# RWKV-7 recurrence and exact-GELU MLP on one core: one hand-written table of single-engine steps in place of loops and calls

## The chip, the cores and the metric

The kernel runs on one core of a Trainium2 chip. The metric is the device time of one execution, in microseconds (us), the median over runs. The engines of the core are named as in the profile: PE (TensorE matmul) with PEld (its weight loads), DVE (VectorE), ACT (ScalarE), POOL (GpSimd), and the queue SP (SyncE), which in this kernel issues nearly all DMAs.

## The reference

A recurrence over 768 time steps, for 4 batches and 8 heads with a state of 40 by 40, and then an MLP on its output. Cut to what matters:

```python
for t in range(S):                                   # S = 768; B, H, D = 4, 8, 40
    y[:, :, t] = einsum('bhd,bhde->bhe', rt, state)
    Sa = einsum('bhde,bhe->bhd', state, at)
    state = state * wt[:, :, None, :] - einsum('bhd,bhe->bhde', Sa, bt) \
            + einsum('bhd,bhe->bhde', vt, kt)
x = y.transpose(0, 2, 1, 3).reshape(B * S, H * D)    # 3072 x 320
h = x @ w_in                                         # w_in 320 x 2048, w_out 2048 x 320, both float64
out = (0.5 * h * (1 + erf(h / sqrt(2)))) @ w_out
```

## The kernel before, in words

Time is cut into 12 chunks of 64 steps. All arithmetic is float32. A chunk c has these parts.

- **Inputs.** SP loads w, a, b, k, v and r of the chunk. Chunks 0 to 2 (for b and k 0 to 3) come as rows of 160 bytes and are turned by PE against an identity; later chunks come in pairs and are turned by DVE.
- **Decays** (`logs`, `sums`). ACT takes the logarithm of w, PE sums it along time (`wT_ps` and `cum`), ACT takes exponentials. DVE and POOL scale a, b and k by them (`scale_a`, `scale_b`, `scale_k`).
- **Masked products** (`make_N`, `make_A`, `make_RV`). 32 small matmuls each on PE, a mask on DVE.
- **The inverse of a triangular matrix.** For chunk 0 by squarings on PE (`squares`). For the others N goes to DRAM (`make_N`, L617), comes back as blocks (L672), POOL inverts the blocks of 32 column by column (`start_inverse`, L680 and L682), the result goes to DRAM (`store_inverse`, L694) and back (`fetch_inverse`, L704 and L708). DVE turns a block of it (`turn_corner`, L780), and PE makes the off-diagonal block in two products, J and its second half (`corner`, `joined`).
- **The state.** `make_av` and `make_X` (PE, tile XA), copies, `make_sa` (PE, tile S), a mask on DVE, `make_QY` (PE, the state products), `outputs` (DVE additions into the state and into xt, the MLP's input, with some rows of xt moved by eleven small DMAs on SP), `turn_state` and `make_y2`.
- **The MLP.** `mlp` makes, for each quarter of the hidden width, two groups of ten matmuls and one exact GELU on ACT into the tile gt (L986, L988). The second product is plain in chunks 0 to 2 (L1003) and from chunk 3 on takes seven half-size products for eight (`seven`, L939), with additions on DVE. The result is stored from the tile os.

The weights are float64, and the chip has no such arithmetic: `to_float` builds a float32 from the two 32-bit words. There are 26 pieces, ten of `w_in` (128 x 512) and sixteen of `w_out` (128 x 320). Each takes bit operations on DVE and one ACT operation (L321 to L326) and is ended either by DVE (L329, L330) or by ACT and POOL together (L332 to L335). The words of `w_in` are landed in the tiles of `w_out`, of gt and in a spare tile (`first_load`, L379 to L388), those of `w_out` in several places (`second_load`, L403), some of them issued by ACT's queue.

The order of the instructions of each engine is the order of the program's calls, and each engine takes its own in that order: an instruction that waits holds everything behind it on its engine or queue. For chunks 0 and 1 the calls are written out one by one; for chunks 2 to 11 a loop (L1229) makes them. MLP pieces of the chunk before are put between by `fill()`, each a quarter of the hidden width (20 matmuls of 256 columns each for x), or one product. Five matmul groups on constants (`keep`) and three before the first input (`warm`) compute nothing that is used. All PE results go through a ring of four PSUM tiles (`duo`), used strictly in turn. Most small matmuls have line L110, that of the helper `mm`; flips have L461, masks L577.

```python
    def fill(n=1):                                   # L1017
        while n and pieces:
            if next(pieces[0], "end") == "end":
                pieces.pop(0)
            else:
                n -= 1
...
    for c in range(2, NCH):                          # L1229, cut
        n, n2 = c + 1, c + 2
        corner(c); make_av(c); make_y2(c); fill(); make_X(c); fill()
        load_next(n2); joined(c); scale_b(n); fill(); make_sa(c)
        ...
        make_QY(c); outputs(c); pieces.append(mlp(c)); fill()
        make_A(n); sums(n2); turn_state(); fetch_inverse(n)
        ...
        make_N(n2); start_inverse(n2, nc.gpsimd); load_kb(n2); load_VR(n2)
```

Of the kernel before, what the change touches and what calls it, by code (L numbers as in the profile page):

```python
# [15 lines left out]

@with_exitstack
def kernel(  # L20
# [12 lines left out]

    nc = tc.nc
# [15 lines left out]
    REST = HP - D  # L83

    const = ctx.enter_context(tc.tile_pool(name="const", bufs=1))
    work = ctx.enter_context(tc.tile_pool(name="work", bufs=1))
    dram = ctx.enter_context(tc.tile_pool(name="scr", bufs=2, space=bass.MemoryType.DRAM))
    psum = ctx.enter_context(tc.tile_pool(name="psum", bufs=4, space=PSUM))

    asked = []  # L90

    def keep(columns):

        asked[:] = [columns]

    def duo(name):
        pt = psum.tile([P, 2, 512], FP32, tag="duo", name=name)
        while asked:
            n = asked.pop()
            mm(pt[:, 0, :n * P], ident, cum_m.unsqueeze(1).to_broadcast([P, n, P]))  # L100
        return pt
# [3 lines left out]

    def head_of(i, x):
        return 2 * i + x
# [5 lines left out]
    def ring(name, n, shape, zero, eng):  # L113
        tiles = []
        for i in range(n):
            t = const.tile(shape, FP32, name=f"{name}{i}")
            if zero is not None:
                eng.memset(zero(t), 0.0)
            tiles.append(t)
        turn = [0]  # L120

        def take():
            turn[0] += 1
            return tiles[(turn[0] - 1) % n]
        return take
# [4 lines left out]
    def whole(t):  # L130
        return t


    def unused(t, eng):
        for x in range(2):
            eng.memset(t[x * HP + BL:(x + 1) * HP, :, BW - BL:D + BL], 0.0)


    NT = 3

    NB = 4
    NS = 3
    paired = {n: const.tile([P, G * H, BW], FP32, name=n + "_pairs") for n in ("a", "v", "r")}
    w_tile = const.tile([P, G * DM + REST], FP32, name="w_tile")


    extra = const.tile([P, 4 * G * H * HP], FP32, name="extra")
    b_rows, k_rows = ([const.tile([P, G * DM + REST], FP32, name=f"{n}_rows{i}") for i in range(2)] for n in "bk")

    def rows(t):  # L150
        return t[:, :G * DM].rearrange("p (g h d) -> p g h d", g=G, h=H)

    raws = {}

    def rows_of(src, c, e):

        return src[G * e:G * (e + 1), :, c * C:(c + 1) * C, :].rearrange("g h t d -> t (g h) d")
# [1196 lines left out]
```

## Time and profile before

| what | value |
|---|---|
| time, three runs | 714.62, 717.1, 721.06 us; median 717.1 |
| span of the profiled execution, first to last instruction | 712.0 us (the page gives no other time for it; the median is 5.1 us above) |
| PE busy | 659.8 us, 93% |
| PEld busy | 574.9 us, 81% |
| DVE busy | 373.2 us, 52% |
| POOL busy | 353.3 us, 50% |
| ACT busy | 229.9 us, 32% |
| mean granted PE clock | 0.965 |
| DMA | 74.25 MB in 287910 packets, 104 GB/s |

How to read it: the page shows one profiled execution. "Busy" is the time in which at least one instruction of the engine was running. The slices row cuts the span into 40 equal parts, each digit the busy share in tenths. In a timeline a row has start and length in us, engine, line, operation, and in brackets how long the engine stood idle before it and what ended that. A PE row of "x40" counts each float32 matmul twice, since it is done in two passes.

### The profile page before, as it was taken

The numbers are of one execution on the slowest core, as the hardware profiler recorded it, in microseconds if no ns is written. First come the engines' busy times: TensorE is split into PE (matmuls) and PEld (weight loads), VectorE is DVE, ScalarE is ACT, GpSimd is POOL, SyncE is SP. The second block draws the span as 40 slices with busy tenths as digits, with TensorE's granted clock in tenths as the row PEclk, the third lists the DMA queues.
The fourth block names the chain that finished last, engine by engine and source line by source line (L and its number), as shares of the span: only waits on it lengthen the run. The fifth ranks groups of instructions, "written<-read, shape, count | busy, mean of one in ns | idle before, by whom it ended". The sixth has DMA issues, their size and how long they took to land.

```text
span 712.0 us, 29566 instructions
## 1 busy us (share of the span) xinstructions
PE 659.8 (93%) x13240; PEld 574.9 (81%) x13240; DVE 373.2 (52%) x484; ACT 229.9 (32%) x306; POOL 353.3 (50%) x796
## 2 busy tenths in 40 slices
PE   7577896789999999999998999999999999999997
PEld 4476685667777877899897798998898898998887
DVE  2325768994262482683582573672771862712303
ACT  5123873453141242242332332333323323111020
POOL 4384458800862862863844823855837818800000
PEclk9777899789999999999999999999999999999999
DMA  9699539764667557557657446647748553120100
GB/s 130 118 168 154 100 99 199 121 129 85 124 121 117 118 102 127 116 100 133 126 94 135 94 94 126 131 90 133 138 83 153 109 102 66 23 51 3 29 9 19
DMA packets 287910, 74.25 MB, mean 104 GB/s; under 512 B 265736, under 2 KB 284456, under 8 KB 287784
## 3 DMA queue, kind: packets, MB, share of 16 engines
q1 hardware_dynamic: 283360, 68.20, 52.5%
q0 software_dynamic: 864, 2.36, 2.0%
q10 hardware_dynamic: 3560, 1.80, 1.3%
q8 instruction: 104, 1.70, 1.1%
q14 instruction: 22, 0.18, 0.1%
HBM read 58.69 MB, written 9.70 MB: 96 GB/s over the span
## 4 chain that ended last, share of the span: by engine, by line
PE 79%; DVE 6%; ACT 3%; DMA 3%; issue 3%; SPq 3%; POOL 2%; ACTq 1%; DVEq 0%; POOLq 0%
PE ph L986 28%; PE po L939 18%; PE po L1003 6%; PE XA L110 5%; PE QY L110 4%; PE J L110 2%; PE S L110 2%; PE sq L110 2%; PE RV_ps L110 2%; PE N_ps L110 2%; SPq L163 2%; PE Y L110 1%; PE tn_ps L461 1%; PE A_ps L110 1%; DMA VR<-in_v_dram 1%
## 5 line engine op out<-in xcount | busy, mean ns | idle before, releaser
L986 PE MATMUL ph<-xt,w_in_sb 64*128 64x256 f32 x1920 | 223.6, 386 | 4.8 <-ACT kT L544 4.8
L986 PEld LDWEIGHTS ph<-xt,w_in_sb 64*128 64x128 f32 x1920 | 185.3, 190 | 30.0 <-ACT kT L544 5.2
L680 POOL TENSOR_TENSOR tmp<-W,Nb 128x126 f32<-128x126 f32 (+22 forms) x310 | 128.3, 414 | 157.8 <-DMA Nb<-N 134.9
L682 POOL TENSOR_TENSOR W<-W,tmp 128x126 f32<-128x126 f32 (+22 forms) x310 | 131.4, 424 | 24.3
L988 ACT ACTIVATE gt<-ph 128x1024 f32<-128x1024 f32 x48 | 49.2, 1024 | 180.7 <-PE ph L986 180.7
L939 PE MATMUL po<-w_out_sb,gt 128*128 128x160 f32 x576 | 82.8, 302 | 1.3 <-DVE gt L959 1.3
L939 PEld LDWEIGHTS po<-w_out_sb,gt 128*128 128x128 f32 x576 | 78.8, 190 | 3.3 <-DVE gt L959 1.5
L1003 PE MATMUL po<-w_out_sb,gt 128*128 128x320 f32 x192 | 53.9, 436 | 0.0
L827 DVE COPY SM<-XA 128x832 f32<-128x832 f32 x10 | 10.3, 1025 | 78.9 <-PE XA L110 78.9
L1003 PEld LDWEIGHTS po<-w_out_sb,gt 128*128 128x128 f32 x192 | 35.7, 190 | 14.7 <-issue 0.3
L836 DVE TENSOR_TENSOR SM<-S,upper 128x832 f32<-128x832 f32 x24 | 23.5, 1019 | 33.9 <-PE S L110 33.9
L794 ACT COPY Js<-J 128x256 f32<-128x256 f32 x11 | 4.1, 373 | 85.4 <-PE J L110 85.4
L810 DVE COPY Tt<-J 32x512 f32<-32x512 f32 x9 | 6.2, 689 | 42.6 <-ACT Tt L810 42.6
L901 ACT COPY st<-apart 128x640 f32<-128x640 f32 x11 | 8.0, 726 | 55.1 <-DVE apart L900 55.0
L939 PE MATMUL po<-extra,half 128*128 128x160 f32 x176 | 25.4, 299 | 0.0
L879 DVE TENSOR_TENSOR st<-QY,st 128x832 f32<-128x832 f32 (+1 forms) x22 | 20.8, 986 | 8.4 <-PE QY L110 8.4
L322 ACT ACTIVATE conv<-conv,rebias 128x320 uint32<-128x320 uint32 (+1 forms) x26 | 15.9, 623 | 28.0 <-DVE conv L321 23.8
L991 DVE TENSOR_TENSOR half<-gt 128x1024 f32<-128x1024 f32 x9 | 11.3, 1260 | 25.8 <-ACT gt L988 25.8
L939 PEld LDWEIGHTS po<-extra,half 128*128 128x128 f32 x176 | 24.2, 190 | 0.0
L110 PE MATMUL XA<-VR,A 64*64 64x104 f32 x768 | 22.5, 270 | 0.0
L577 DVE TENSOR_TENSOR N<-N_ps,upper 128x1024 f32<-128x1024 f32 x12 | 14.7, 1221 | 13.4 <-PE N_ps L110 13.4
L670 POOL MEMSET W<- 128x512 f32 x10 | 5.3, 530 | 32.6 <-DMA inv<-W 32.6
(208 smaller groups left out, 1107.5 us busy)
## 6 DMA issues: line engine op xcount, KB each, us to landing
Nb<-N SPq DMA_DIRECT2D x20, 256.0 KB
VR<-in_v_dram SPq DMA_DIRECT2D x24, 160.0 KB
out_dram<-os SPq DMA_DIRECT2D x48, 80.0 KB
b_rows<-in_b_dram SPq DMA_DIRECT2D x22, 160.0 KB
k_rows<-in_k_dram SPq DMA_DIRECT2D x22, 160.0 KB
N<-N SPq DMA_DIRECT2D x44, 64.0 KB
Tt<-inv SPq DMA_DIRECT2D x44, 64.0 KB
a_pairs<-in_a_dram SPq DMA_DIRECT2D x18, 144.0 KB
```

The source lines that it names most:

```text
L110: nc.tensor.matmul(o, lhsT, rhs, start=first, stop=True, skip_group_check=True)
L163: eng.dma_start(out=t[half(e)].rearrange("p g h d -> p (g h) d")[:, :, :D], in_=rows_of(src, c, e))
L322: nc.scalar.activation(power, power, ACT.Relu, bias=rebias, scale=8.0)
L577: nc.vector.tensor_tensor(to, pt, upper.unsqueeze(1).to_broadcast([P, 2 * G * NP, C]), ALU.mult)
L680: eng.tensor_tensor(t, W[:, :rows, j:j + 1].to_broadcast([P, rows, rest]), Nb[:, j:j + 1, j + 1:].to_broadcast([P, rows, rest]), ALU.mult)
L682: eng.tensor_tensor(W[:, :rows, j + 1:], W[:, :rows, j + 1:], t, ALU.add)
L836: nc.vector.tensor_tensor(SM[:, g], S[g].rearrange("p x i c -> p i x c"), pass_upper.unsqueeze(1).unsqueeze(1).to_broadcast([P, NP, 2, VC] ...
L879: nc.vector.tensor_tensor(given[g][:, :, :, cols], t["QY"][g][:, :, :, cols], given[g][:, :, :, cols], ALU.add)
L939: nc.tensor.matmul(po[:, n, :DM // 2], l_[:, f], r_[:, f], start=f == 0, stop=f == NF // 2 - 1)
L986: nc.tensor.matmul(ph[:, x, s], w_in_sb[half(x), kt, p * P:(p + 1) * P], xt[half(x), kt], start=kt == 0, stop=kt == NK - 1)
L988: nc.scalar.activation(gt[:, 4 * q:4 * q + 4].rearrange("p (x s) t -> p x s t", x=2), ph, ACT.Gelu)
L1003: nc.tensor.matmul(po[:, g], gt[:, f, g * P:(g + 1) * P], w_out_sb[:, f], start=f == 0, stop=f == NF - 1)
```

## The change

Nearly the whole text of the kernel is rewritten. The arithmetic is the same. Each part above is cut into **steps** that run on one engine (or are one DMA group on one queue), a table lists all steps of all chunks in one order, and a loop performs them. A name has the step, the chunk and at times a part: `mh.3.6` is piece 6 of 8 of chunk 3's first MLP product.

- PE: `wT`, `cu` (the two sums), `ta tb tk tv tr` (flips of a, b, k, v, r), `nm am vm` (the products N, A, RV), `qm` (squarings), `jm km` (J and its second half), `av xm` (XA), `sm` (S), `pk pb` (state products), `tm ym`, `mh` (first MLP product, now 10 matmuls to a step where `fill` gave 20), `pm` (a quarter of the second product), `m1` to `m7`.
- DVE: `sb sa` (scaled b, a), `nk ak vk` (masks), `qz qa` (squarings), `tc_` (the turned block), `sc` (mask of S), `oa om od` (state, xt, decayed state), `s1` to `s4`, `e2 e4 e5 e6`, and of the conversions `cp cm cs cv`. The number of a conversion step is its unit: 0 to 9 are `w_in`, 10 to 25 `w_out`.
- ACT: `lg ew en ec`, copies, `ge` (GELU), `ce cl cn` of the conversions.
- POOL: `ic` (columns of the inverse, in groups), `iz`, `sk` (scaled k), `cg` (end of a conversion).
- DMA, a last letter giving the queue (s for SP if none): `L` steps (`Lw La Lb Lk LV Lv Lr` inputs, `Lf Lfe Lf5` words of `w_in`, `Ls` units of `w_out`), `Ns Nl` (N out and back), `Is If Ij` (inverse out and back), `ox` (rows of xt), `so` (store).

The core of the diff: the loop, the `keep` calls, the pools with rotating tiles and the generators go; in come fixed tiles, four PSUM tiles handed out in the order in which they come free, and the table.

```diff
-    psum = ctx.enter_context(tc.tile_pool(name="psum", bufs=4, space=PSUM))
-    def keep(columns):
-        asked[:] = [columns]
-    def duo(name):
-        pt = psum.tile([P, 2, 512], FP32, tag="duo", name=name)
-        while asked:
-            n = asked.pop()
-            mm(pt[:, 0, :n * P], ident, cum_m.unsqueeze(1).to_broadcast([P, n, P]))
-        return pt
-    for c in range(2, NCH):
-        ...
-    fill(1000)
+    banks = [psum.tile([P, 2, 512], FP32, name=f"bank{i}") for i in range(4)]
+    idle, held, left = list(range(4)), {}, {}
+    def take(name, readers=1):
+        held[name] = idle.pop(0)
+        left[name] = readers
+        return bank(name)
+    def drop(name):
+        left[name] -= 1
+        if not left[name]:
+            idle.append(held.pop(name))
+    @step
+    def mh(c, p):
+        q, s = p // 2, p % 2
+        ph = (bank if s else take)(f"ph{c}_{q}").rearrange("p x (s t) -> p x s t", s=2)
+        for kt in range(NK):
+            for x in range(2):
+                nc.tensor.matmul(ph[:, x, s], w_in_sb[half(x), kt, p * P:(p + 1) * P], xt[half(x), kt],
+                                 start=kt == 0, stop=kt == NK - 1)
+    for token in order(NCH, NS):
+        perform(steps, token)
```

The landing places of the words: `w_in`'s first half in the tiles of `w_out` and its second half in gt, as before, but its last unit now in xt; `w_out`'s units in the tiles of `w_out`, gt and the second row tiles of b and k:

```diff
+    def first_home(kt, part):
+        if part == 0:
+            return flat_out[:, kt * LW:(kt + 1) * LW]
+        return flat_xt[:, :LW] if kt == NK - 1 else flat_gt[:, kt * LW:(kt + 1) * LW]
+    def second_home(f):
+        n = 2 * DM
+        if f < 8:
+            return flat_out[:, f * n:(f + 1) * n]
+        if f in (8, 14):
+            return b_rows[1][:, :n].bitcast(UINT32)
+        if f in (9, 15):
+            return k_rows[1][:, :n].bitcast(UINT32)
+        if f == 13:
+            return flat_out[:, 7 * n:8 * n]
+        at = NF // 2 * TB + (f - 10) * n
+        return flat_gt[:, at:at + n]
```

The table begins so, and a later stretch (chunks 5 and 6) reads:

```
Lw.0 lg.0 La.0 Lf.0.1.1 Lb.0 pads_a.0 identity pads_rows.0 first_ones.0 pads_w.0 pads_extra.0
pads_extra.1 sums_mask cu.0 ec.0 sb.0 Tt_zero pads_a.1 upper_mask wT.0 tb.0 sn.0 ew.0 ta.0 sa.0 nm.0 nk.0
Lw.1 first_ones.1 iz.1 qt lg.1 cu.1 pads_VR.0 pads_w.1 pads_VR.1 pads_rows.1 bias_set Lf.1.1.0 Lf.0.0.0
Lf.0.1.0 Lf.1.1.1 Lf.0.0.1 Lf.1.0.0 Lf.1.0.1 Lk.0 Lfe.0 pads_extra.2 qi qm.0 cl.2 warm_set cp.0
warm_first cp.1 cm.0 ce.0 ce.1 qc.0 ec.1 cs.0 qz.0 qm.1 qc.1 cv.0 cm.1 cl.1 cn.1 qa.1 qz.1 cm.2 La.1
Lfe.1 Lr.0 Lb.1 Lf.2.1.1 Lf5.0.1 Lf.3.1.1 Lf5.0.0 Lf.2.1.0 Lf.3.0.1 Lf.3.0.0 LV.0 Lf.2.0.1 Lf.3.1.0
Lf.2.0.0 pads_r.0 sk.0.p wT.1 qm.2 cs.1 cp.2 sb.1 ew.1 cn.2 ce.2 cl.3 cs.2 cg.1 cm.3 cg.2 qc.2 tk.0 tb.1
...
Ls.14 Nl.2.1 La.3 Nl.2.0 Lw.3 ge.0.2 cn.22 cl.22 cp.22 ce.22 cs.22 cg.22 ge.0.3
...
e2.4 e4.4 e5.4 e6.4 LV.7 LV.6
ox.5.0 nm.7 av.6 ym.6 If.6.1 Ij.6.0 nk.7 Ij.6.1 La.8 If.6.0 tc_.6 yc.6 mh.5.2 jm.6 xm.6 jc.6 km.6 kt0.6
mh.5.3 xc0.6 kt1.6 xc1.6 sm.6 sc.6.1 mh.5.6 sc.6.0 mh.5.7 mh.5.0 mh.5.1 mh.5.4 mh.5.5 so.4.1 Ns.7.0
```

Counted over the program: matmuls 6715 (before 6720), SP's DMAs 756 (746), ACT's DMAs 6 (16), ACT table loads 41 (34), POOL's two-tensor operations 719 (711), DVE's scalar-operand operations 128 (136). The three warm matmuls stand behind the first squaring.

## The prediction

> **What bounds the kernel now.** I read the page's busy shares first, then the table of stretches, the timelines of TensorE (PE) and of the SP queue, and last the round trip of one chunk's inverse.
>
> ```profile
> span 712.0 us, 29566 instructions
> PE 659.8 (93%) x13240; PEld 574.9 (81%) x13240; DVE 373.2 (52%) x484; ACT 229.9 (32%) x306; POOL 353.3 (50%) x796
> ...
> PE   7577896789999999999998999999999999999997
> ...
> PEclk9777899789999999999999999999999999999999
> ```
>
> PE is busy for 93% of the span, and both the idle time and the low clock lie in the first nine of the 40 slices. The table of stretches (time, PE, PEld, DVE, ACT, POOL, granted clock, DMA share, GB/s) cuts it at 157.0 us, where the corner product J of chunk 2 starts:
>
> ```profile
> 0.00:18.00 18.00, 13.54 (x224) 8.55 (x225) 5.04 (x6) 10.59 (x11) 8.91 (x34) 1.00 1.04 130
> 27.00:41.00 14.00, 9.64 (x273) 8.56 (x264) 3.30 (x5) 2.31 (x4) 4.44 (x16) 0.51 0.76 149
> 107.00:125.00 18.00, 12.18 (x204) 10.16 (x202) 15.08 (x26) 5.98 (x9) 15.71 (x32) 0.94 1.01 200
> 107.00:157.00 50.00, 37.17 (x626) 29.75 (x623) 44.15 (x83) 21.94 (x30) 32.22 (x70) 0.86 0.79 147
> 0.00:157.00 157.00, 119.83 (x2912) 97.79 (x2913) 94.89 (x149) 74.30 (x98) 88.68 (x188) 0.86 0.76 134
> 157.00:708.00 551.00, 540.00 (x10328) 477.10 (x10328) 278.25 (x336) 155.64 (x208) 264.61 (x608) 1.00 0.52 96
> ```
>
> After 157 us PE does 540.0 us of work in 551.0: only 11.0 us can be had there. Before it, PE idles for 37 us, and much of its 119.8 busy us is at half clock:
>
> ```profile
> 38.44 1.97 PE L461 MATMUL kT_ps<-ident,extra 128*128 128x128 f32 x8
> 66.27 1.61 PE L110 MATMUL S<-SM,Tt 64*64 64x104 f32 x61
> 98.58 4.59 PE L986 MATMUL ph<-xt,w_in_sb 64*128 64x256 f32 x40
> 113.58 1.09 PE L461 MATMUL kT_ps<-ident,extra 128*128 128x128 f32 x8
> 123.94 7.34 PE L986 MATMUL ph<-xt,w_in_sb 64*128 64x256 f32 x40 [4.76 <-ACT kT L544]
> 157.02 0.74 PE L110 MATMUL J<-L,N 32*32 32x32 f32 x64 [1.95 <-DVE L L780]
> ```
>
> The same eight transposes take 1.97 us in the half-clock stretch and 1.09 at full clock. At full-clock prices what precedes 157.0 is 86 us: eight MLP pieces of 2.23 (L986: 4.59 for two, overlapping), 4.5 for a quarter of the second MLP product, 8.5 for the squarings, 9.4 for six products 104 wide (1.57 each), 6 for four state products, 5 for four running sums, 2.6 for corners, and 32 flips and masked products of about 1.0. So the head loses 157 - 86 = 71 us. In its last 50 us DVE is busy for 44.15 (converting `w_out`); in its first 90 the weights are late:
>
> ```profile
> 32.63 2.62 SPq L385 DMA_DIRECT2D w_out_sb<-in_moe_w_in_dram  x4
> 88.21 8.34 SPq L379 DMA_DIRECT2D spare_raw<-in_moe_w_in_dram  x8
> ```
>
> The first word of `w_in` is asked for at 32.6 us, the last at 96; DVE, ACT and POOL cannot convert before.
>
> **The change, part by part.** *Five `keep` fillers go*: 0.39, 0.49, 2.00, 0.91 and 0.49 us in the PE timeline, 4.3 in all. *The start-up warm matmuls move* from 1.6 us to behind the first squaring: same 5.36 us at most. *Half-length pieces* have the same matmuls; no price. *SP takes ten DMAs from ACT's queue*: the SP rows of L403 average 0.47 us, so +4.7 us of issue, in a stretch where SP is nearly always issuing; it is inside the walk below. *Four more weight pieces go to POOL* (two operations of 0.9 us each at 320 columns, from 1.4 at 512), 7 us there, off DVE.
>
> *ACT loads its tables 41 times, not 34.* The row is 1.28 us, and the activation starts 0.02 us after the load: +9.0 us on an engine that is 32% busy, mostly under PE work; without that cover at most 9.0. The Trainium skill, "ScalarE: Activation LUTs", section "What ACT_TABLE_LOAD costs", adds a drain of 1.38 us per switch, which would make it 18.6; these rows show no such drain, and the sum does not use it.
>
> *The new order* is the real change. I walked its head engine by engine, each step starting when its engine and its inputs are free, with durations from the rows of before, and DMA at 125 GB/s for 160-byte rows (130 in the first 18 us) and 190 for weights (200 in 107 to 125 us):
>
> - SP issues most of `w_in`'s first half right behind the first w, a, b and w. The first unit is complete after four row loads (1.28 MB, 10.2 us) and eight weight blocks (1.79 MB, 9.4 us), with some 2 us until the first bytes move: 22 us. DVE's order puts `cp.0` ahead of `qz.0`, so the squarings of chunk 0 wait for it: second squaring at 25 us (before 28.6).
> - b of chunk 1 now comes behind k, a, r and another 0.26 MB of weights: 10.2 + 1.3 us more, at 34; `sb.1` stands ahead of `qa.2` and holds DVE about 5 us. Fourth squaring at 38 (before 45.7).
> - V of chunk 0 is behind 1.6 MB of weights (8.4 us) and its own 2.6: 45. The squarings end at 43, `vk.0` at 51, the copies that S needs at 56: S of chunk 0 starts there (before 66.3). Units 0 to 6 were converted in the gaps of the squarings.
> - b of chunk 2 lands at 68 behind N, V, w, r and the last of `w_in`, and holds DVE for 3 us. `om.0.1` ends at 71; SP then issues six xt copies (4.3 us), V and three `w_out` units (4.2) and five copies (3.4), so xt of chunk 0 is whole at 85 and the first MLP runs from 85 to 106 (before 98.6 to 131.3).
> - The inverse of chunk 1 now stands behind six weight pieces on POOL (2.8 us each) and its N, stored by SP behind `nk.1` at 44, is back at 60: 29.3 us of columns (before 34.1 to 63.4) and two more pieces and a memset inside them, 6 us, end at 96. Store, fetch and DVE's queue (`cv.25` ends at 109.6) give J of chunk 1 at 110 (before 81.0). That is the price of the earlier weights; it is covered as long as the MLP lasts until about then.
> - From there PE goes J, its second half at 112 (ACT's copy waits behind `ce.18`), a quarter of the product to 117.2, S to 118.8, a quarter to 123.3. DVE ends the conversions ahead of `sc.1` at 119.4 and `sc.1` at 123; the state products of chunk 1 end at 126.3.
>
> A walk without contention and with a warm clock is a lower estimate. The first five steps start unwarmed, and PE waits between 60 and 85 us; one half-clock spell of 5 to 10 us costs 2.5 to 5. I add 4.7: the point is reached at 131 us. Bounds: 118 (DVE and DMA as walked, but the two b waits gone, 5 and 3 us) and 157 (no gain at all).
>
> The Trainium skill, "TensorE: Matmul & The Clock Gate", Part 1, says that the default state is throttled and that some 3.4 us of sustained work releases it. The trace agrees: half clock in 27 to 41 us after idle gaps. By that rule the moved warm matmuls leave the first flips cold and cost some 4 us, inside the bounds above.
>
> At that point the new order has done 4.5 us more of MLP and 7.8 less of chunks 2 and 3 than the old one at 157.0, so 540.0 + 3.3 = 543.3 us of PE work remain.
>
> *Idle behind it.* The inverse leaves PE at N, goes through DRAM and POOL, and comes back for J:
>
> ```profile
> 522.91 1.16 PE L110 MATMUL N_ps<-aT,nT 40*64 40x64 f32 x64
> 536.99 0.24 POOL L680 TENSOR_TENSOR tmp<-W,Nb 128x31 f32<-128x31 f32 x1 [11.38 <-DMA Nb<-N]
> 569.21 1.64 POOL L694 DMA_DIRECT2D inv<-W  x2 [0.30 <-POOL W L682]
> 578.04 0.71 DVE L780 STREAM_TRANSPOSE L<-Tt 128x512 f32<-128x512 f32 x1 [0.76 <-DMA Tt<-inv]
> ```
>
> That is 55.8 us from N to the turned block (mean of eight chunks 56.4). Counting PE work between `nm.c` and `jm.c` in the new table gives 57.9, 63.6, 57.1, 55.5, 60.7, 57.0, 54.8, 60.8 and 52.7 us for chunks 3 to 11. A stall at one J lengthens the next chunk's distance (its N is already out), so a trip of 56.4 stalls 0.9 + 1.6 + 3.7 = 6.2 us. J of chunk 2 waits 2.5 in the walk. With part of the old 11.0 I take 16 us of idle; bounds 8 and 40.
>
> Sum: 131 + 543.3 + 16 + 4.0 (the old tail behind 708) = 694.3 us of span. The page gives the profiled execution a span of 712.0; the median of the runs is 5.1 above it, their lowest 2.6. With 5.1: **699 us**.
>
> **Rivals.** *Gain eaten in the head.* The recurrence's own inputs queue behind weights, and DVE, in order, stalls on each: b of chunk 1, V, b of chunk 2, then every `w_out` unit. For: DVE has 101 us of work up to the last weight unit, so every wait of it counts. Against: the walk already carries 8 us of such waits. At 150 us instead of 131 the time is 718, no change.
>
> *The inverse's round trip becomes the bound (slower).* SP issues for about 17 of every 20 us between 180 and 580 us, and in the new table `If` stands behind `ox`, `Lr` and the N stores of the next chunk. If the trip grows to 66 us, the stalls are 8.1 + 8.9 + 1.6 + 3.7 + 5.3 + 5.9 + 13.3 = 46.8 in place of 6.2: 740 us. From a trip of about 62 us (27.1) it has eaten the gain. Against: the old order's 56.4 holds SP waits too.
>
> *The order does not matter*: DVE's conversions alone set 157. DVE is busy for 94.9 of those 157 us, so there is room; I count it with the first rival.
>
> **How the numbers follow.** Forecast 0.70, head rival 0.14, round trip 0.12, other mishaps 0.04. The measurement can tell about 1% (7 us) from no change. The forecast's own range is 678 (118, 8 idle) to 712. Faster: most of the forecast and little else, 0.72; same: the head rival, 0.12; slower 0.16. The range reaches from 676 over the head rival to 722.
>
> **What would show it.** Right: `w_in` words from about 5 us, S of chunk 0 before 60, the first MLP from 85 to 90, state products of chunk 1 done before 136, PE idle behind that under 20 us. Wrong: DVE idle at `sb.1` or `sb.2` for over 10 us; J waiting on DVE's turned block for 3 us or more in most chunks.

## The result and the profile after

The changed kernel takes 771.2 us (median of four runs, 769.8 to 772.9); the kernel before took 717.8 beside it. The ratio is 1.074, with a 95% interval of 1.070 to 1.079: slower by 7%, where 699 us had been forecast. In this document a time is the median of all runs of a kernel, and a ratio leaves out slow runs, those over 1.5% above the kernel's fastest. The profiled execution of the changed kernel took 769.8 us, with a span of 768.1.

The page of the changed kernel, the lines that answer to those shown of before:

```profile
span 768.1 us, 29570 instructions
PE 667.6 (87%) x13230; PEld 586.8 (76%) x13230; DVE 381.5 (50%) x476; ACT 242.4 (32%) x321; POOL 383.5 (50%) x804
...
PE   4677789997996999988959899969969897989997
...
PEclk9779998998998999998987999989997997999999
```

PE does the same work, but the nearly unbroken row of nines that the kernel before had from the tenth slice on is gone. A slice below nine comes again and again up to slice 36, and the clock is low in most of these places or right behind them. The stretches (time, then busy time of PE, PEld, DVE, ACT, POOL, granted clock, DMA share, GB/s), cut where the state products of chunk 1 end, first of the changed kernel:

```profile
0.00:138.20 138.20, 104.41 (x2587) 86.94 (x2587) 91.87 (x142) 73.78 (x103) 73.84 (x141) 0.90 0.79 151
138.20:768.10 629.90, 563.23 (x10645) 499.82 (x10644) 289.66 (x334) 168.57 (x218) 309.62 (x664) 0.94 0.47 85
```

and of the kernel before, cut at the same event:

```profile
153.70:712.00 558.30, 541.38 (x10334) 477.73 (x10332) 281.50 (x343) 157.10 (x210) 264.61 (x608) 0.99 0.52 96
```

So the head really is 15.5 us shorter (138.2 against 153.7). Behind it the changed kernel needs 629.9 us in place of 558.3: PE idles for 66.7 us (4.3 of them the tail) in place of 16.9, and its busy time is 22 us longer. From there to its last matmul PE's clock is at half for 68 us (3.4 before), and PE is busy in 52 of these. What PE waited for (total us, times, longest):

```profile
PE bank L193 <- DVE conv L960: 31.9, 7, 8.8
...
PE bank L193 <- DMA T<-inv_blocks: 8.2, 2, 5.8
...
PE bank L1184 <- DMA xt<-xt: 6.3, 2, 5.0
```

The first line is J waiting for the turned block of the inverse, the second its second half waiting for the block that `Ij` fetches: 40.1 us. The kernel before lost 4.1 us at J:

```profile
PE J L110 <- DVE L L780: 4.1, 2, 2.1
```

The trip of chunk 10, from N to J, in the timelines of PE, SP, POOL, DVE and PE again:

```profile
563.47 1.11 PE L193 MATMUL bank<-aT,nT 40*64 40x64 f32 x64
572.33 1.92 SPq L886 DMA_DIRECT2D Tt<-inv_blocks  x4
574.36 2.46 SPq L1293 DMA_DIRECT2D out_dram<-os  x4
576.86 5.48 SPq L426 DMA_DIRECT2D r_pairs<-in_r_dram  x8
582.94 2.03 SPq L851 DMA_DIRECT2D N_blocks<-N  x4
591.64 0.24 POOL L872 TENSOR_TENSOR tmp<-W,Nb 128x31 f32<-128x31 f32 x1 [18.38 <-DMA Nb<-N_blocks]
627.53 1.64 POOL L879 DMA_DIRECT2D inv_blocks<-W  x2 [0.30 <-POOL W L874]
640.90 0.71 DVE L960 STREAM_TRANSPOSE conv<-Tt 128x512 f32<-128x512 f32 x1 [11.08 <-DMA Tt<-inv_blocks]
641.76 0.74 PE L193 MATMUL bank<-conv,N 32*32 32x32 f32 x64 [3.23 <-DVE conv L960]
```

N is masked at 565.9 and goes out at 582.9. In the 17 us between, SP stands at the fetch of chunk 9's inverse, which POOL hasn't stored yet, then issues a result and eight pieces of r. POOL idles for 18.4 us meanwhile, DVE stands 11.1 us at the turned block and PE 3.2 at J. From the start of the mask to the end of the turned block the trip takes 77.0 us here, 67.4 in the mean of chunks 5 to 11. In the kernel before that mean is 54.8. Of the 12.6 us between the two means, 5.6 lie between the mask and N's store, 2.5 between the store and the first column, 2.5 in the columns and 2.1 between the last column and the end of the turned block. So N's store is the largest part, and less than half.

The chain of work that ended last moved with it. Changed kernel first, then the version of experiment 1, which has the old order in chunks 3 to 11:

```profile
PE 36%; POOL 26%; SPq 15%; issue 9%; DMA 8%; DVE 3%; ACT 1%; POOLq 0%; DVEq 0%; ACTq 0%
```

```profile
PE 74%; SPq 7%; POOL 5%; issue 5%; DMA 4%; DVE 3%; ACT 2%; ACTq 0%; DVEq 0%; POOLq 0%
```

With the old order PE itself is three quarters of the chain. With the new one POOL, which is mostly the columns of the inverse, and SP's issues are 41%.

### The profile page after: what moved, and what is told of

It reads as the page before. It is cut to its first block, busy times and chain, and to the rows that moved or that the text cites. A ratio compares the mean times of both kernels' runs of the same rounds, so it can differ in the third digit from the quotient of the medians.

```text
span 768.1 us, 29570 instructions
## 1 busy us (share of the span) xinstructions
PE 667.6 (87%) x13230; PEld 586.8 (76%) x13230; DVE 381.5 (50%) x476; ACT 242.4 (32%) x321; POOL 383.5 (50%) x804
## 4 chain that ended last, share of the span: by engine, by line
PE 36%; POOL 26%; SPq 15%; issue 9%; DMA 8%; DVE 3%; ACT 1%; POOLq 0%; DVEq 0%; ACTq 0%
PE bank L1184 13%; POOL W L874 12%; PE bank L193 11%; POOL tmp L872 11%; PE bank L1223 9%; SPq L426 3%; DMA Nb<-N_blocks 3%; DMA inv_blocks<-W 3%; PE bank L1300 2%; SPq L1293 2%; SPq L851 1%; SPq L886 1%; SPq L429 1%; SPq L1132 1%; PE bank L696 1%
## 5 line engine op out<-in xcount | busy, mean ns | idle before, releaser
L1184 PE MATMUL bank<-xt,w_in_sb 64*128 64x256 f32 x1920 | 234.2, 399 | 7.2 <-DMA xt<-xt 6.3
L1184 PEld LDWEIGHTS bank<-xt,w_in_sb 64*128 64x128 f32 x1920 | 194.5, 198 | 35.1 <-issue 7.8
L874 POOL TENSOR_TENSOR W<-W,tmp 128x126 f32<-128x126 f32 (+22 forms) x341 | 158.4, 464 | 26.7
L1189 ACT ACTIVATE gt<-bank 128x1024 f32<-128x1024 f32 x48 | 48.6, 1023 | 153.0 <-PE bank L1184 149.2
L1223 PE MATMUL bank<-w_out_sb,gt 128*128 128x160 f32 x576 | 83.1, 301 | 0.1
L1223 PEld LDWEIGHTS bank<-w_out_sb,gt 128*128 128x128 f32 x576 | 79.1, 190 | 2.7 <-DVE st L1111 1.0
L1300 PE MATMUL bank<-w_out_sb,gt 128*128 128x320 f32 x192 | 55.4, 446 | 0.0
L1300 PEld LDWEIGHTS bank<-w_out_sb,gt 128*128 128x128 f32 x192 | 36.7, 195 | 15.7 <-issue 1.3
L1061 DVE TENSOR_TENSOR SM<-bank,upper 128x832 f32<-128x832 f32 x24 | 23.6, 1018 | 34.2 <-PE bank L193 34.2
L1223 PE MATMUL bank<-extra,conv 128*128 128x160 f32 x176 | 25.5, 299 | 0.0
L1223 PEld LDWEIGHTS bank<-extra,conv 128*128 128x128 f32 x176 | 24.4, 190 | 0.0
L1078 ACT COPY st<-bank 128x1024 f32<-128x1024 f32 x11 | 11.1, 1012 | 39.3 <-PE bank L193 36.4
```

Source lines behind the costliest of these rows:

```text
L874: nc.gpsimd.tensor_tensor(W[:, :rows, j + 1:], W[:, :rows, j + 1:], t, ALU.add)
L1061: nc.vector.tensor_tensor(SM[:, g], pair_of(f"S{c}_", g).rearrange("p x i c -> p i x c"), pass_upper.unsqueeze(1).unsqueeze(1).to_broadcas ...
L1184: nc.tensor.matmul(ph[:, x, s], w_in_sb[half(x), kt, p * P:(p + 1) * P], xt[half(x), kt], start=kt == 0, stop=kt == NK - 1)
L1189: nc.scalar.activation(gt[:, 4 * q:4 * q + 4].rearrange("p (x s) t -> p x s t", x=2), bank(f"ph{c}_{q}").rearrange("p x (s t) -> p x s t", ...
L1223: nc.tensor.matmul(po[:, n, :DM // 2], l_[:, f], r_[:, f], start=f == 0, stop=f == NF // 2 - 1)
L1300: nc.tensor.matmul(po[:, g, :DM], gt[:, f, g * P:(g + 1) * P], w_out_sb[:, f], start=f == 0, stop=f == NF - 1)
```

## The experiments

The main theory, T: in the new table the inverse's round trip has been lengthened, by steps that stand ahead of it on SP, and PE's order leaves it no room. The rivals: the price lies in the clock, in the head, on POOL, or in the order of PE, DVE and ACT. "Table" is the new kernel's, "the loop's order" that of the kernel before, written in steps. Ratios are to the kernel before, run beside each version. Experiments 1, 2, 5, 7 and 9, and all of 6 but its first, also leave out two tiny steps, `one_set` and `one_log`, whose tile nothing else reads.

### 1. The loop's order for chunks 3 to 11

From step `mh.2.6` on, the table is replaced by the steps in the loop's order; one chunk of PE's order as an example:

```diff
-jm.9 xm.9 mh.8.4 mh.8.5 mh.8.1 mh.8.2 km.9 mh.8.3 sm.9 mh.8.6 mh.8.7 vm.10 am.10 pk.9 pb.9 ...
+jm.9 av.9 ym.9 mh.8.0 mh.8.1 xm.9 mh.8.2 mh.8.3 km.9 mh.8.4 mh.8.5 sm.9 mh.8.6 mh.8.7 vm.10 pk.9 pb.9 ...
```

> The new table up to step mh.2.6, and behind it the steps of chunks 3 to 11 in the order of the loop of the kernel before. The end of the first state product of chunk 1 stays at 138 us. Theory T (the inverse's round trip, nk to tc_, has been lengthened from 54 us to 58 to 77 us by what stands ahead of N's store on SP): the trip of chunks 4 to 11 goes back to 52 to 59 us, the idle time of PE behind 138 us falls from 62 to 20 to 30 us (chunks 2 and 3 are still those of the new table) and the half clock from 72 to 25 us, so 138 + 563 - 22 + 25 + 4 = 708 us, between 700 and 722. Rival R1 (the one-step grain, the new PSUM order or the slower columns on POOL lengthen the trip, not the order): the trip stays over 60 us in most chunks and the time over 750 us.

Measured: 715.4 us, ratio 0.9955 (0.9914 to 0.9997); the mean trip is 54.9 us. Its slices and its second stretch:

```profile
PE   4779878988899799999999999999999999999997
```

```profile
139.00:711.50 572.50, 546.36 (x10652) 483.04 (x10644) 282.94 (x333) 158.65 (x211) 294.60 (x665) 0.99 0.51 93
```

The holes are gone. One-step grain, landing places, half-length pieces and free PSUM banks are all still in, so they aren't the cause: the order of the steps of chunks 3 to 11 costs 56 us. And the new head is worth next to nothing. It ends 14.7 us earlier, but behind it PE is busy for 5.0 us more and idle for 9.2 us more (26.1 in place of 16.9); of the 26.1, 9.8 are waits at J of chunks 2 and 3.

### 2. N later on SP, in the loop's order

```diff
-nm.6 nk.6 Ns.6.0 Ns.6.1 iz.6 Nl.6.0 Nl.6.1 Lb.6 Lk.6 LV.6 ...
+nm.6 nk.6 iz.6 Lb.6 Lk.6 LV.6 Ns.6.0 Ns.6.1 Nl.6.0 Nl.6.1 ...      # chunks 5 to 11
```

> The version with the loop's order (715.4), in which N's store and load back of chunks 5 to 11 are put behind the loads of b, k and VR of the same chunk on SP; nothing else is changed. That is 5 to 6 us later, 3 us in chunk 5. Theory T (in the steady part the trip is as long as PE's distance from nm to jm, so its length sets the period): trips of 59 to 62 us in place of 54 to 56, PE waits 3 to 5 us at J in most of the seven chunks, in all 20 to 35 us, and with half-clock spells behind the waits the time is 735 to 755. Rival R4 (a wait at J is made good by work that follows sooner, PE has slack in the steady part): 713 to 722, no half clock.

Measured: 777.2 us, ratio 1.0774 (1.0696 to 1.0853). N was delayed by more than was meant: it left 15.1 us after the mask in place of 1.7, and the trip became 71.6 us. PE's wait for the turned block, all chunks:

```profile
PE bank L189 <- DVE conv L956: 66.3, 10, 9.5
```

Seven moved groups on one queue, nothing else, bring back the whole loss: PE waits 54 us at the J of these seven chunks, and half clock behind 139 us goes from 14 to 82 us. T's direction is shown here, and R4 falls: N 13.4 us later, seven times, is 94 us, and 62 of them come out as time. The steady part has a few us of slack in each chunk, about 4.6 by these two numbers, and most of what is lost isn't made good.

### 3. N by POOL's queue, in the new table

```diff
-Ns.6.1 so.3.1 so.3.0 Ns.6.0 Ij.5.1 Ij.5.0 Lw.7 Nl.6.0 Nl.6.1 ...
+Ns.6.1.p so.3.1 so.3.0 Ns.6.0.p Ij.5.1 Ij.5.0 Lw.7 Nl.6.0.p Nl.6.1.p ...      # chunks 2 to 11
```

> Only the queue of N's store and of its load back (Ns, Nl of chunks 2 to 11) is changed, from SP to POOL, the engine that waits for them; the table is the same. Theory T: N's store goes out 2 to 4 us after nk in place of 3 to 19, the trip falls to 52 to 60 us in chunks 4 to 11, PE's waits at J fall from 40 us to under 15, and with the half clock behind them the time falls by 40 to 65 us, to 705 to 730. Rival R2 (POOL's own columns, 27 to 31 us a chunk, and the distance nm to jm set the trip): POOL, which now also issues six DMAs a chunk, is no earlier, and the time stays at 760 to 780 us.

Measured: 747.7 us, ratio 1.0376 (1.0283 to 1.0468); the profiled one of its runs took 739.6, with a mean trip of 60.1 us. The waits at J of chunks 3 to 11 are gone, one at the second half is left (4.5 us), and xt now costs 10.3. That is under half of the 56 us: T names a part of the loss, and not all.

### 4. N ahead on SP, in the new table (two versions)

First, Ns and Nl of chunks 3 to 11 right behind nk, with the fetch of chunks 6 and 9 behind them:

> The new table, with one queue's order changed: on SP N's store and load back (Ns, Nl of chunks 3 to 11) stand right behind the mask nk, ahead of the loads, of so and (chunks 7 and 10) of the fetch of the inverse of the chunk before. No DMA changes its queue, and no other engine its order. Theory T: N's store goes out within 4 us of nk, the trip falls to 52 to 60 us in chunks 4 to 11, as far as or further than with POOL as the issuer (57 to 65 us, 747.7), because POOL issues nothing more; time 715 to 745. Rival R3 (the gain of the version with POOL as the issuer came from emptying SP, whose other steps were late): the time stays above 755.

Measured: 850.7 us, ratio 1.1785 (1.1699 to 1.1871). This order does more than move N: Nl of chunks 4 and 11 came ahead of the columns of chunks 3 and 10, which so waited for the next chunk's N and inverted that (PE idle 33 and 28 us at their J). So it says nothing of T, except that the fetch of chunk 6, now behind the next N, left SP 28 us after the inverse was done. With the fetch ahead of N, and the next chunk's N behind the columns:

> The new table, chunks 3 to 11: on SP Ns stands right behind nk and Nl right behind Ns (in chunks 4 and 11 behind the last columns of the chunk before), and the fetch If and Ij stays ahead of them where it was (of chunks 5, 6 and 9 the last part of it is moved forward by a few steps); so and loads move behind. This mends the version in which chunks 3 and 10 read the next chunk's N and the fetch of chunks 6 and 9 stood behind the next N. Theory T: trips of 53 to 60 us in chunks 5 to 11, PE waits under 3 us at J, 715 to 745. Rival R3 (N's place on SP is not what lengthens the trip; the rest of the table's order is): 755 or more.

Measured: 775.9 us (766.2 to 782.5 over its four runs), ratio 1.0713 (1.0627 to 1.0799). No gain, as R3 forecast. In the profiled execution, the longest of the four, N left 1.0 us after the mask in place of 7.7, but the fetch started 10.0 us after the last column in place of 5.2, and the mean trip was 65.4 us. So N's place on SP alone is not what makes the table slow: the wait moved to another station of the same queue.

### 5. SP's whole order, in the new table

Only SP's steps of chunks 3 to 11 are permuted, for instance

```diff
-Lr.9 Lw.9 Ns.8.0 Ns.8.1 If.7.0 If.7.1 Nl.8.0 Nl.8.1 so.5.0 Lk.8 Ij.7.1 so.5.1 Ij.7.0 Lkt.9 La.9 ...
+Lr.9 If.7.0 If.7.1 Ns.8.0 Ns.8.1 Ij.7.1 Ij.7.0 Lkt.9 Nl.8.0 Nl.8.1 so.5.0 so.5.1 Lv.9 Lbt.9 ...
```

> The new table; PE, DVE, ACT and POOL keep their orders, and the order of SP alone is changed for chunks 3 to 11: each of its steps stands where its inputs come up, by the durations of the profiled runs, with the fetch of the inverse, N's store and load and the rows of xt ahead of loads and stores of results. Theory T2 (SP's order as a whole lengthens the trip: putting N ahead alone only handed the wait to the fetch, 17 us late in chunk 10, and to the rows of xt, 7.8 and 9.2 us of PE): trips of 53 to 61 us in chunks 4 to 11, PE's idle time behind 138 us under 40 us in place of 62, time 725 to 748. Rival R6 (the order of PE, DVE or POOL is at fault, SP's queue only follows): 755 or more.

Measured: 758.9 us, ratio 1.0563 (1.0497 to 1.0629); the mean trip is 64.5 us. Twelve us back, not thirty: the time is R6's and not T2's, for this one order of SP. N now leaves 5.0 us after the mask (7.7 in the table as it was), but the fetch starts 7.8 us after the last column (5.2), and the turned block starts 3.3 us after the fetch's last issue (2.2).

### 6. The trip off SP, and POOL's order

All of it on POOL:

```diff
+... ic.6.28.31 Is.6.0.p Is.6.1.p If.6.0.p If.6.1.p Ij.6.0.p Ij.6.1.p iz.7 Ns.7.0.p Ns.7.1.p Nl.7.0.p Nl.7.1.p ic.7.0.4 ...
```

> The new table; the whole round trip of the inverse of chunks 3 to 11 is taken off SP: N's store and load (Ns, Nl) and the fetch (If, Ij) are issued by POOL, which makes the inverse, in the order Is, If, Ij, Ns, Nl, columns. SP keeps the inputs, the rows of xt and the stores of results. Theory T3 (in the new table the trip is lengthened by SP's waits at each of its stations, and only at those): mean trip of chunks 5 to 11 54 to 59 us in place of 67 (60 with Ns and Nl alone on POOL), PE's idle time behind 138 us under 35 us, time 718 to 738. Rival R7 (POOL's queue, with ten more DMAs a chunk, becomes the line that holds the trip, or PE waits for other things than the trip in this table): 742 to 765.

Measured: 767.6 us, ratio 1.0706 (1.0626 to 1.0786), mean trip 65.6 us: R7's side, a little above its range. One stall shows how waits hand each other on. Rows of POOL, ACT, DVE and PE:

```profile
504.58 1.54 POOL L732 TENSOR_TENSOR k_rows<-k_rows,part 128x640 f32<-128x640 f32 x1
```

```profile
506.16 0.70 ACT L685 ACTIVATE part<-bank 128x640 f32<-128x640 f32 x1 [15.10 <-POOL k_rows L732]
```

```profile
507.08 0.32 DVE L1174 TENSOR_TENSOR os<-os 128x160 f32<-128x160 f32 x1 [13.77 <-ACT os L1266]
```

```profile
506.92 3.30 PE L1221 MATMUL bank<-extra,gt 128*128 128x160 f32 x11 [14.54 <-ACT part L685]
```

The scaled k (`sk.8`) stands behind the inverse and its fetch on POOL. ACT wants to overwrite the tile that it reads and waits 15.1 us; an addition on DVE waits for ACT's next step, and PE for the PSUM bank that ACT has still to read. So POOL's order was exchanged alone, in both directions. Into the loop's order:

> The version with the loop's order (715.4), with POOL's order taken from the new table (the scaled k of chunks 5, 6 and 8 behind the columns of the inverse, of chunk 9 ahead of the last group); all other engines as they were. Theory T4 (POOL's order is part of the cause): mean trip of chunks 5 to 11 over 57 us, time 722 to 740. Rival R8 (POOL's order matters nothing): 712 to 719.

Measured: 725.8 us, ratio 1.0105 (1.0047 to 1.0163), mean trip 57.4 us: 10 us worse than the loop's order, so T4 is right here: POOL's order alone is worth that much. Into the new table:

> The reverse: the new table (771.2) with POOL's order taken from the version with the loop's order (each scaled k behind the first eight columns); all other engines as they were. Theory T4: mean trip 62 to 65 us in place of 67.4, time 745 to 763. Rival R8: 765 to 775.

Measured: 772.6 us, ratio 1.0753 (1.0692 to 1.0813), mean trip 70.2: nothing gained, as R8 forecast. A late `sk` hurts a good order and mending it doesn't help a bad one. Then POOL's better order with N on POOL, and SP by readiness:

> The new table; PE, DVE and ACT keep their orders. POOL has the loop's order and issues N's store and load (chunks 3 to 11) ahead of its columns; SP's other steps stand in order of readiness. Theory T5 (the two queues on the way of the inverse, together, make the trip long): mean trip 55 to 59 us, time 715 to 737. Rival R9 (the orders of PE, DVE and ACT themselves make N, the turned block and the inputs late, so no order of SP and POOL brings the trip back): mean trip 60 us or more, time 740 to 765.

Measured: 757.0 us, ratio 1.0517 (1.0453 to 1.0581), mean trip 65.4, in R9's range. N leaves 0.3 us after the mask, but the fetch 12.5 us after the last column. In chunk 7, from 422.9 to 445.6 us, SP issues almost without a pause: b, w, k, V, rows of xt and r ahead of `If`. Last, with the whole trip on POOL:

> The new table; PE, DVE, ACT and the rest of SP as they are; POOL has the loop's order (scaled k behind the first eight columns) and issues the whole trip of chunks 3 to 11: Is, If, Ij, then Ns, Nl, then the columns. Theory T5 (the queues on the way of the inverse make the trip long): mean trip 54 to 59 us, time 718 to 740. Rival R9 (the orders of PE, DVE and ACT make N or the turned block late whatever the queues do): mean trip over 61 us, time 745 to 770.

Measured: 764.8 us, ratio 1.0665 (1.0601 to 1.0729), mean trip 68.1, R9's range again. SP's queue no longer carries the trip, but POOL has no room left: chunk 5's columns run from 290.1 to 328.2 us, then store, fetch and N take 23 us with their landings, and chunk 6's start at 351.0, 61 us after chunk 5's.

### 7. More distance for the trip

Four steps of the first MLP product (three in chunk 5), with the GELUs that they complete, go from behind J to ahead of it; SP, POOL and DVE keep their orders.

```diff
-jm.9 xm.9 mh.8.4 mh.8.5 mh.8.1 mh.8.2 km.9 mh.8.3 sm.9 ...
+mh.8.4 mh.8.5 mh.8.1 mh.8.2 jm.9 xm.9 km.9 mh.8.3 sm.9 ...
```

> The new table; SP, POOL and DVE keep their orders; in chunks 3 to 11 four steps of the first MLP product (three in chunk 5), with the GELUs that they complete, are moved from behind J to ahead of it. The distance from nm to jm grows from 53 to 64 us to 62 to 72 us by the matmul prices; the trip's DMAs are untouched. Theory T (the trip costs time against this distance only): waits at J fall from 40 to under 12 us, time 730 to 752, though the trip stays over 62 us. Rival R10 (the steps from J to the state products lose their cover, and PE waits there as long as it did at J): 760 or more.

Measured: 772.7 us, ratio 1.075 (1.0676 to 1.0824). The waits for the turned block fell to 7.4 us (3.5 of them in chunk 2), as T asked, and the time did not move:

```profile
PE bank L1180 <- DMA xt<-xt: 10.0, 3, 5.6
...
PE bank L189 <- DVE late L698: 8.2, 2, 5.7
PE bank L189 <- DVE conv L956: 7.4, 3, 3.5
```

PE idles for 56 us behind 139 us all the same (62 in the table), and half clock rose to 85 us. At J the idle time fell from 32 to 5 us. It rose from 10 to 19 us in the steps from there to the state products, most of it at S, and from 3 to 13 at the product RV, which waits mostly for the turned v. R10's time holds, and its place for a part. T in its narrow form falls: the wait at J is where the lateness shows, not the only place where it is paid.

### 8. The clock, and the head

Four matmuls on constants ahead of each J that waited:

```diff
+warm.4 warm.4 warm.4 warm.4 jm.9 xm.9 ...
```

> The table is the same, but ahead of each jm from chunk 2 on that waited stand four matmuls of 128 by 512 on constants, which compute nothing that is used. They fill 4 x 0.43 x 2 = 3.4 us of each stall at J. Theory C (a stall of 4 to 9 us is followed by a spell of half clock, which costs as much again): where they fit into the stall they cost nothing, and the stall that is left is under 4 us in most chunks; half clock behind 138 us falls from 72 to under 30 us and the time by 10 to 20 us, to 750 to 760. Rival (the half clock is no result of these stalls, or the trip sets every chunk's end whatever PE's clock): half clock stays over 50 us and the time is 768 to 790.

Measured: 766.7 us, ratio 1.0676 (1.0598 to 1.0754). Half clock behind 139 us falls from 68 to 24 us (the 72 of the text above counts the last spell, behind the last matmul), as C had it, and the time by 4.5 us, between the two forecasts. The fillers themselves explain why it is so little. The nine groups take 33.6 us of PE, and its idle time fell by only 25, so about 8 us of them did not fit into a stall. PE's other work became 12 us shorter (562 to 550), and what the fillers left of those 12 us is about the gain. How much of the higher clock would be kept without the fillers' own time is not shown. The warm matmuls moved to the start of the table:

> The steps warm_set and warm_first (matmuls on constants) are moved from between the first two squarings to the start of the table. Theory H (in the new head they run at half clock for 4.8 us in the path of chunk 0's squarings and hold cv.0): qm.1 begins at 26 to 27 us in place of 30.0, the state product of chunk 1 ends 1 to 4 us before 138.2, and the time is 0 to 5 us shorter. Rival: the words of the weights set the head (they land at 21 us and are converted one after the other), so the first state product of chunk 1 ends within 1 us of 138.2 and the time is 768 to 774.

Measured: 771.8 us, ratio 1.0764 (1.0662 to 1.0865): no change. The second squaring does start 2.3 us earlier,

```profile
27.67 3.64 PE L190 MATMUL bank<-turned,st 32*32 32x64 f32 x128 [6.39 <-DVE st L936]
```

against 29.98 in the changed kernel, but now at half clock (3.64 us in place of 1.99). A spell of 20.5 us follows at 46.3 us, J of chunk 1 comes at 123.6 (122.6), and nothing is left of the gain.

### 9. What the new head can give

In the loop's order the head's gain is lost at J of chunks 2 and 3. Started earlier on SP:

> The version with the loop's order (715.4), in which the inverses of chunks 2 and 3 are started earlier as well: Ns.2 right behind nk.2, Nl.2 right behind Is.1, the columns of chunk 2 between the last conversions that POOL ends, Is.2 issued by POOL, If.2 and Ij.2 ahead of so.0, and Ns.3 and Nl.3 ahead of Lr.4. Theory T: J of chunks 2 and 3 no longer waits (5.6 and 4.2 us), the half clock behind these waits goes (13.6 us, about 6 us of time), so 711.5 - 10 - 6 = 696 us of span, 694 to 704 as a time, faster than both kernels. Rival R5 (what the head wins is given back elsewhere, whatever is started earlier: the conversions, xt or the state chain take over in chunks 2 and 3): 709 to 718.

Measured: 719.0 us, ratio 0.9957 (0.9916 to 0.9999), a little above R5's range and far from T's. J of chunk 2 no longer waits, but J of chunk 1 comes at 130.4 in place of 123.6. In this order columns of chunk 2 stand ahead of a conversion on POOL, and DVE stood for it, with the turned block behind:

```profile
125.82 0.49 DVE L610 SCALAR_TENSOR_TENSOR w_out_sb<-conv 128x320 f32<-128x320 f32 x1 [7.48 <-POOL conv L632]
...
129.56 0.71 DVE L956 STREAM_TRANSPOSE conv<-Tt 128x512 f32<-128x512 f32 x1
```

With POOL's queue for N of chunks 2 and 3, and the columns behind the conversions:

> The version with the loop's order (715.4); N of chunks 2 and 3 goes out and back by POOL's queue (Ns.2 behind the conversion cg.14, Nl.2 behind cg.16, Ns.3 and Nl.3 behind nk.3), so nothing is put ahead of the fetch of chunk 1 on SP; the columns of chunk 2 stand before and behind cg.22; the fetch of chunk 3 and N of chunk 4 stand ahead of Lr.5. Theory T: J of chunk 1 stays at 123 to 124 us (in the version with SP as the issuer tc_.1 came 7 us later), J of chunks 2 and 3 doesn't wait, half clock behind 139 us under 7 us, span 694 to 702, time 697 to 706. Rival R5 (chunks 2 and 3 find another wait of the same size): 710 to 718.

Measured: 716.3 us, ratio 0.9947 (0.9913 to 0.9981). The state of chunk 3 is ready at 245 us, 10 us earlier than in experiment 1, and the end is where it was, as R5 forecast. PE then waits in chunks 4 and 11 (2.2 and 2.8 us, each with a half-clock spell). One piece of the MLP ahead of J there:

```diff
-jm.4 jc.4 av.4 ym.4 yc.4 mh.3.0 mh.3.1 ge.3.0 xm.4 ...
+mh.3.0 mh.3.1 ge.3.0 jm.4 jc.4 av.4 ym.4 yc.4 xm.4 ...      # chunks 4, 5, 11
```

> The version with the loop's order and N of chunks 2 and 3 by POOL's queue (716.3; span 711.8), in which one piece of the MLP (20 matmuls of 256 columns, 4.5 us) is put ahead of J in chunks 4, 5 and 11, where PE still waited there (2.2 us in chunk 4, 2.8 us in chunk 11, 6.8 and 3.4 us of half clock behind them). Theory T: the distance from nm to jm is 4.5 us longer in these chunks, the two waits and their half clock go, so 711.8 - 5 - 5 = 702 us of span, 700 to 711 as a time. Rival R5 (another wait of the same size comes up): 712 to 719.

Measured: 712.4 us, ratio 0.9914 (0.9879 to 0.9949), span 708.0: 0.9% below the kernel before (interval 0.5 to 1.2%), a small difference, but the best of all. The waits at J of chunks 4 and 11 are gone, as T had it, but the median lies at the lower edge of R5's range and not in T's. Its stretch behind the head, first experiment 1, then this version:

```profile
139.00:250.00 111.00, 97.03 (x1868) 79.36 (x1862) 46.01 (x52) 29.71 (x36) 68.58 (x162) 0.94 0.60 107
```

```profile
139.00:250.00 111.00, 105.67 (x2264) 86.79 (x2256) 54.29 (x61) 34.91 (x41) 72.52 (x162) 1.00 0.58 110
```

PE is busy for 8.6 us more of the same 111 us, at full clock. By the end 3.5 of them are left (708.0 against 711.5, one execution each; the medians are 3.0 apart).

### The versions side by side

Mean over chunks 5 to 11; "late" is from the end of nk to N's store, "columns" from POOL's first to last, "fetch" from the last column to the first `If`. Idle and half clock are PE's, from 139 us (before: 153.7) to its last matmul. The time is a median; all other columns are of the one profiled execution.

| version | time | trip | late | columns | fetch | idle | half clock |
|---|---|---|---|---|---|---|---|
| piece ahead of J (9) | 712.4 | 57.0 | 3.8 | 33.0 | 5.1 | 19 | 7 |
| loop's order (1) | 715.4 | 54.9 | 1.7 | 32.5 | 5.3 | 22 | 14 |
| loop's order, early N on POOL (9) | 716.3 | 56.8 | 3.5 | 32.8 | 5.2 | 19 | 17 |
| before | 717.8 | 54.8 | 2.1 | 32.1 | 6.2 | 13 | 3 |
| loop's order, early N on SP (9) | 719.0 | 55.1 | 1.9 | 32.5 | 5.3 | 20 | 10 |
| loop's order, new POOL order (6) | 725.8 | 57.4 | 2.5 | 32.9 | 5.4 | 28 | 27 |
| table, N by POOL (3) | 747.7 | 60.1 | 0.4 | 33.4 | 6.1 | 41 | 34 |
| table, N by POOL, SP by readiness (6) | 757.0 | 65.4 | 0.3 | 32.6 | 12.5 | 47 | 68 |
| table, SP by readiness (5) | 758.9 | 64.5 | 5.0 | 33.9 | 7.8 | 54 | 68 |
| table, trip on POOL, loop's POOL order (6) | 764.8 | 68.1 | 7.3 | 36.4 | 5.8 | 58 | 72 |
| table, fillers (8) | 766.7 | 65.4 | 6.0 | 34.1 | 4.9 | 37 | 24 |
| table, trip on POOL (6) | 767.6 | 65.6 | 4.3 | 34.6 | 6.3 | 63 | 68 |
| table (the changed kernel) | 771.2 | 67.4 | 7.7 | 34.6 | 5.2 | 62 | 68 |
| table, warm matmuls first (8) | 771.8 | 67.1 | 7.5 | 34.8 | 4.9 | 58 | 72 |
| table, loop's POOL order (6) | 772.6 | 70.2 | 9.1 | 36.2 | 5.2 | 69 | 68 |
| table, longer distance (7) | 772.7 | 67.0 | 6.2 | 34.5 | 5.2 | 56 | 85 |
| table, N behind nk, fetch ahead (4) | 775.9 | 65.4 | 1.0 | 34.9 | 10.0 | 66 | 79 |
| loop's order, late N (2) | 777.2 | 71.6 | 15.1 | 36.0 | 4.5 | 72 | 82 |
| table, N first on SP (4) | 850.7 | 80.1 | 0.9 | 33.4 | 13.6 | 134 | 147 |

Time and trip rise together, roughly, over all of them. That alone doesn't say which drives which; experiment 2 shows that a longer trip makes the time longer, experiment 7 that room at J alone doesn't make it shorter. What is shown: the order of chunks 3 to 11 costs 56 us, N's two steps on SP account for up to 24 of it, and no order of SP or POOL that was tried brings the table below 747. What stays open: which part of the orders of PE, DVE and ACT holds the rest. The orders of SP, PE, DVE and ACT can't be exchanged alone, in either direction, because the engines would wait for each other in a circle. With SP's order of the loop, for instance, the load `Lb.7` stands behind `Ns.7`, which needs the mask `nk.7`; in the table DVE has `sb.7`, which needs that load, ahead of `sn.7`, which `nk.7` needs. Only POOL's order could be exchanged alone.

## Why the prediction was wrong, step by step

- **The head.** The walk's mechanism was right and its size 7 us off: 138.2 us where 131 was taken, inside the bounds of 118 and 157. The first words land at 21.1 us (forecast 22), and `sb.1` does not wait (the walk had 5 us). But the first warm matmuls run between the first two squarings, 4.82 us at half clock, and the second squaring is at 30.0 (25; with the warm matmuls moved away it starts 2.3 us earlier), the fourth at 44.7 (38), S of chunk 0 at 67.5 (56) and the first MLP at 96.2 (85). J of chunk 1 comes at 122.6 (110). The bounds for the cold start sat on the total and not on the step where it falls.
- **PE work left, 543.3 us.** As an amount of work it was right: in the loop's order 546.4 us are busy with 14 us of them at half clock. As a time it was 20 us short, 563.2: the sum put the clock behind the head at nothing, though it expected J to wait there. PE was busy for 52 us at half clock, and half of that, 26 us, is an estimate of what it cost.
- **Idle behind it, 16 us, bounds 8 and 40: the step that failed.** It was 62.4. The sum took the old order's trip of 56.4 us for the new one, though its own rival says that in the new table `If` stands behind `ox`, `Lr` and the next chunk's N stores. Distances were counted in the new order, and the trip in the old. That trip measured 67.4 (54.8 in the kernel before, by the same measure), and J and its second half waited 40.1 us in place of the 8.7 in the sum. Even the true trip set against the distances would not have been the whole account: in experiment 7 more distance took the waits at J away and left the time. The range up to 712 us also used neither upper bound of the sum; 157 and 40 together give 749.
- **The tail, 4.0, and the gap from span to time, 5.1**: 4.3 and 1.7. The terms are 138.2 + 563.2 + 62.4 + 4.3 + 1.7 = 769.8, the profiled time.
- **The round-trip rival** named the mechanism, the place and nearly the size: from a trip of 66 us it made 46.8 us of stalls where 40.1 were measured at J and its second half. Its 740 us (56.6 us of idle time) lacked the 7 us of the head, the 20 us of half clock and 6 us of other waits. It had a chance of 0.12; "SP issues for 17 of every 20 us" was the reason to give it more. "The old order's 56.4 holds SP waits too" was no argument: a wait in one order says nothing of another.
- **The head rival** (150 us in place of 131) was wrong as worded, but its effect came in another way: with the steady part mended, the head that ends 15 us earlier is worth next to nothing (spans of 711.5 and 712.0; ratio of the times 0.9955).
- **"What would show it"**: DVE stood nowhere for 10 us at `sb.1` or `sb.2`; J waited 3 us or more in chunks 2, 3, 6, 9 and 10 and its second half in chunk 5. The sign for "wrong" was the right one, though in half of the chunks and not in most. Of the signs for "right" only the first came: words of `w_in` are asked for from 4.0 us, but S of chunk 0 (67.5), the first MLP (96.2), the state products of chunk 1 (138.2) and the idle time (62.4) all lie beyond their marks.

## What to carry to other kernels

A loop that leaves an engine, goes through DRAM and another engine, and comes back is priced in the order that will run it. Walk the queue that carries it through one steady chunk, with each DMA's issue time and what it waits for, before its old length is used again. Where several in-order queues are each nearly full, relieving one moves the wait to the next: put the whole order, then one queue or engine where it can be exchanged alone, back into the order that is known to run, and look at the chain that ended last. A head that ends earlier is worth only what the first waits behind it leave.

## What the hardware showed

Half-clock spells have lengths of 3.4, 6.8, 10.2, 13.7, 17.1 or 20.5 us, whole multiples of 3.4 (the first version of experiment 4, with stalls of 33 and 28 us, has 34.1 and 30.7 as well; a spell at the end of a trace is cut off). In the changed kernel each PE stall of 4.8 to 7.1 us came with 6.8 or 10.2 us of half clock, the one of 8.8 with 13.7; the spell begins before the stall has ended or with its end. The Trainium skill, "TensorE: Matmul & The Clock Gate", Part 1, gives windows of about 3.4 us, and these lengths agree. Its section "HAM oscillation — how this bites in real kernels" puts the loss at half of the throttled time, which would be 34 us here, an estimate. In this trace PE was busy in 52 of the 68 us, half of which is 26, beside the 22 us by which its busy time grew.

POOL's columns are slowed beside some additions on DVE. Rows of POOL from the first version with the whole trip on POOL (experiment 6):

```profile
480.48 0.41 POOL L870 TENSOR_TENSOR tmp<-W,Nb 128x121 f32<-128x121 f32 x1
480.97 1.28 POOL L872 TENSOR_TENSOR W<-W,tmp 128x121 f32<-128x121 f32 x1
482.32 1.25 POOL L870 TENSOR_TENSOR tmp<-W,Nb 128x110 f32<-128x110 f32 x1
...
486.34 0.40 POOL L872 TENSOR_TENSOR W<-W,tmp 128x108 f32<-128x108 f32 x1
```

Four operations in a row take 1.25 to 1.28 us in place of 0.41. In DVE's timeline just those five us hold four additions of 128x1024:

```profile
480.59 1.38 DVE L1174 TENSOR_TENSOR conv<-gt 128x1024 f32<-128x1024 f32 x1
```

The Trainium skill, "GPSIMD Engine Reference", section 1, says that the engine shares its SBUF interfaces with VectorE, with contention where DVE reads two SBUF inputs; the rows agree and put it at three times the duration. It may be one reason why the columns take 32 us in some orders and 36 in others; no run separates it from others. A group of four DMAs of N took 2.0 us to issue on SP (chunk 10 of the changed kernel, 582.94 us) and 2.6 on POOL (at 339.09 us in the last version of experiment 6).
